# Strassen's seven products for the output product of eight token tiles in a fused attention and bilinear feed-forward kernel

## The chip, the cores and the metric

The kernel runs on one core of a Trainium2 chip. The metric is the device time of one execution in microseconds. A program on one core has single runs; a run counts as slow when it lies over 1.5% above the fastest run of the same kernel. A median quoted here is over all runs, as recorded; where one of them was slow, the median without it stands beside it. Ratios and verdicts (faster, same, slower at 2%, or unclear) come from the fast runs alone, of the same rounds on the same chip, with a 95% interval.

## The reference

```python
scores = scale * np.matmul(q, k.transpose(0, 1, 3, 2))     # q, k, v: 8 batches, 8 heads, 576 positions, 64
mask_local = (rel >= 0) & (rel < 32)                       # heads 0 to 3
mask_strided = (rel >= 0) & (pos[None, :] % 32 == pos[:, None] % 32)   # heads 4 to 7
... # masked softmax
x = attn_out.transpose(0, 2, 1, 3).reshape(4608, 512)
a = x @ w_a                                                # 512 -> 1536
b = x @ w_b
out = (a * b) @ w_out                                      # 1536 -> 512, float32
```

## The kernel before

The 4608 tokens are worked off in 9 tiles of 512. A tile has 16 slots: 12 for blocks of 128 hidden features (two products, then the multiply into `pf`), and 4 for 128 tokens each of the output product. The attention of the next batches is strewn into the slots as steps S (scores), V (values and normalising, which writes `xT`, the input of the products) and D (transposes of k and q on VectorE, then transfers on the sync engine's queue). The kernel fixes the order of each engine's instructions itself (`manual_schedule`); the order below is therefore part of the design. PSUM is the memory that matmuls write to; it is used here in banks of 512 float32 columns.

```python
def ffn_ab(t, f, mid, ab=None):
    ...                                     # 4 + 4 matmuls of 512 columns into two PSUM banks
    a_sb = fsb.tile([128, TTOK], F32, tag="a_sb", name="a_sb")
    nc.scalar.copy(a_sb, ab[0])
    nc.vector.tensor_mul(pf[:, f, :], a_sb, ab[1])

def ffn_y(t, j, mid):
    ...
        y = psum4["mm"].tile([128, n], F32, tag="mm", name="mm")
        for f in range(FD):                 # 12 matmuls of 512 columns
            nc.tensor.matmul(y, lhsT=pf[:, f, 128 * j:128 * (j + 1)], rhs=wo_sb[:, f, c0:c0 + n],
                             start=(f == 0), stop=(f == FD - 1))
        ...                                 # copy to SBUF, one store of 128 rows

# a V step from batch 2 on: ScalarE makes 1/sum, VectorE multiplies it into xT
nc.scalar.activation(r, sums, ACT.Ln)
nc.scalar.activation(r, r, ACT.Exp, scale=-1.0)
for j in range(2):
    ...
    nc.vector.tensor_mul(dst[:, W * half:W * (half + 1)], o[:64, j, :W], r[:, j])

# the slots of the attention steps from batch 3 on, and of the transposes from batch 4 on
LATER = {-2: "S0", -1: "S1", 0: "V0", 1: "S2", ... 10: "V5", 11: "S7", 12: "V6", 13.5: "V7"}
gs = ... (3, 5, 7, 9, 11, 12, 13, 14, 15, 17)
```

The softmax here doesn't subtract the row's maximum and nothing guards it: scores larger than these inputs give would overflow.

Of the kernel before, what the change touches and what calls it, by code (L numbers as in the profile page):

```python
# [7 lines left out]
F32 = mybir.dt.float32  # L8
BF16 = mybir.dt.bfloat16
I16 = mybir.dt.int16  # L10
ALU = mybir.AluOpType
# [12 lines left out]
PW = 344  # L24
VW = 128
WCH = (0, 2, 5, 8, 10, 12)


@with_exitstack
def kernel(  # L30
# [10 lines left out]
    nc = tc.nc  # L41
    B, H, S, D = q.shape
    assert (B, H, S, D) == (8, 8, 576, 64)
    scale = 1.0 / (D ** 0.5)
    d_model = H * D
    n_tok = B * S
    d_ff = moe_w_a.shape[1]
    KD = d_model // 128
    FD = d_ff // 128
    TTOK = 512  # L50
    NT = n_tok // TTOK
    HL = H // 2
    W = S // 2

    const = ctx.enter_context(tc.tile_pool(name="const", bufs=1))
    wp = ctx.enter_context(tc.tile_pool(name="weights", bufs=1))
    nat = ctx.enter_context(tc.tile_pool(name="nat", bufs=1))
    sb = ctx.enter_context(tc.tile_pool(name="sb", bufs=3))
    fsb = ctx.enter_context(tc.tile_pool(name="ffn", bufs=2))
# [3 lines left out]
    psum4 = {}  # L63
# [90 lines left out]
                             rhs=nc.const_aps.tensor(1.0, [128, 224], BF16), start=True, stop=True)  # L154

    cur = {}
    xT = const.tile([128, KD, n_tok], BF16)
    wa_sb = wp.tile([128, KD, d_ff], BF16)
    wb_sb = wp.tile([128, KD, d_ff], BF16)
    wo_sb = wp.tile([128, FD, d_model], BF16)  # L160

    tl = {}

# [2 lines left out]


    nats = {}

    def load_qk(b, strided, heads=range(HL), names="kq"):  # L170
        for nm in names:
            src = {"k": k, "q": q}[nm]
            if b < FIRST_D:
                n, R, h0 = (NP, RS, HL) if strided else (96, RL, 0)
                if (b, nm, strided) not in nats:
                    nats[b, nm, strided] = nat.tile([n, HL, R, D], BF16, tag=f"{nm}{R}", name=f"{nm}{R}", bufs=1)
                t = nats[b, nm, strided]
                hs = slice(heads[0], heads[-1] + 1)
                nc.gpsimd.dma_start(out=t[:, hs], in_=src[b, h0:h0 + HL].rearrange("h (p r) d -> p h r d", r=R)[:, hs])
            elif strided:  # L180

                t = nat_s[nm]
                n = 32 if b == FIRST_D else YS
                for h in heads:
                    nc.gpsimd.dma_start(  # L185
                        out=t[32 * h:32 * h + n],
                        in_=bass.AP(tensor=src.tensor, offset=(b * H + HL + h) * S * D,
                                    ap=[[RS * D, n], [YS * RS * D, 3], [1, RS * D]]))
            else:
                if 0 in heads:  # L190
                    nats[b, nm, strided] = nat.tile([128, NY, D], BF16, tag=f"{nm}l", name=f"{nm}l")
                t = nats[b, nm, strided]
                for h in heads:
                    nc.gpsimd.dma_start(out=t[32 * h:32 * h + 32],  # L194
                                        in_=src[b, h].rearrange("(i y) d -> y i d", y=32))
            nats[b, nm, strided] = t
# [127 lines left out]
    ps = {}  # L324
# [102 lines left out]
    def step_VT(b, u):  # L427

        c, half, M, n, G = unit(u)
        p = ps.pop((b, u))  # L430
        o = psum4["o"].tile([128, 2, 512], F32, tag="o", name="o")
        for i in range(G):
            for j in range(2):
                if c < 2:
                    vt = vl_buf[b % 2][:, (2 * c + j) * 6 + 3 * half + i]
                else:
                    vt = vs_buf[b % 2][:, 2 * (c - 2) + j, 4 * half + i]
                nc.tensor.matmul(o[:, j, i * n:(i + 1) * n], lhsT=vt, rhs=p[:M, j, i * n:(i + 1) * n], start=True, stop=True)  # L438

        r = sb.tile([128, RS * 4 * D], BF16, tag="xr", name="xr", bufs=2)[:64, :4 * W].bitcast(F32)  # L440
        r = r.rearrange("p (j w) -> p j w", j=2)
        if c < 2:
            sums = o[64:, :, :W]
        else:

            sums, r = (t.rearrange(e, p=NP) for t, e in ((o[64:, :, :W], "d j (g p) -> d j p g"), (r, "d j (p g) -> d j p g")))
        nc.scalar.activation(r, sums, ACT.Ln)  # L447
        nc.scalar.activation(r, r, ACT.Exp, scale=-1.0)  # L448
        for j in range(2):
            dst = xT[64 * j:64 * j + 64, c, S * b:S * (b + 1)]  # L450
            if c < 2:
                nc.vector.tensor_mul(dst[:, W * half:W * (half + 1)], o[:64, j, :W], r[:, j])  # L452
            else:
                nc.vector.tensor_mul(dst.rearrange("d (p r) -> d p r", r=RS)[:, :, G * half:G * (half + 1)],  # L454
                                     o[:64, j, :W].rearrange("d (g p) -> d p g", p=NP), r[:, j])
# [10 lines left out]
    def X_e(b, c):  # L466
        n = LW if c < 2 else NP
        tp = held.pop((b, "x", c))
        tv = tp.rearrange("d (g p) -> d g p", p=n)
        dst = xT[:, c, S * b:S * (b + 1)]  # L470
        if c >= 2:
            dst, tv = dst.rearrange("d (p r) -> d p r", r=RS), tv.rearrange("d g p -> d p g")
        else:
            tv = tp
        if (b, c) == (0, 3):
            nc.vector.tensor_copy(dst[:, :NP // 2], tv[:, :NP // 2])
            nc.scalar.copy(dst[:, NP // 2:], tv[:, NP // 2:])
        else:
            nc.scalar.copy(dst, tv)
# [30 lines left out]

    pfs = {}

    def ab_mm(t, f, ab, kks, mid=None, first=0, last=KD - 1):
        for w, ps_ in zip((wa_sb, wb_sb), ab):
            if mid and ps_ is ab[1]:
                mid()
            for kk in kks:
                nc.tensor.matmul(ps_, lhsT=w[:, kk, 128 * f:128 * (f + 1)], rhs=xT[:, kk, TTOK * t:TTOK * (t + 1)],  # L518
                                 start=(kk == first), stop=(kk == last))

    def ffn_ab(t, f, mid, ab=None):
        if f == 0:
            pfs[t] = fsb.tile([128, FD, TTOK], BF16, tag="pf", name="pf", bufs=1)
        pf = pfs[t]
        if ab is None:
            ab = [psum4["mm"].tile([128, TTOK], F32, tag="mm", name="mm") for _ in range(2)]
            if f == 0:

                late = 1 if t == 1 else 3
                ab_mm(t, f, ab, [kk for kk in range(KD) if kk != late], last=-1)  # L530
                ab_mm(t, f, ab, [late], first=-1, last=late)
            else:
                ab_mm(t, f, ab, range(KD), mid)
        a_sb = fsb.tile([128, TTOK], F32, tag="a_sb", name="a_sb")
        nc.scalar.copy(a_sb, ab[0])  # L535
        nc.vector.tensor_mul(pf[:, f, :], a_sb, ab[1])  # L536
        return pf[:1, f, :1]

    def ffn_y(t, j, mid):
        pf = pfs[t]  # L540

        c0 = 0
        for z, n in enumerate((256, 128, 128) if (t, j) == (NT - 1, 3) else (d_model,)):
            y = psum4["mm"].tile([128, n], F32, tag="mm", name="mm")
            for f in range(FD):
                nc.tensor.matmul(y, lhsT=pf[:, f, 128 * j:128 * (j + 1)], rhs=wo_sb[:, f, c0:c0 + n],  # L546
                                 start=(f == 0), stop=(f == FD - 1))
                if f == FD // 2 - 1:
                    mid()
            y_sb = fsb.tile([128, n], F32, tag="y_sb", name="y_sb", bufs=3)  # L550
            act = t < NT - 1 or (j + z) % 2 == 1
            (nc.scalar.copy if act else nc.vector.tensor_copy)(y_sb, y)  # L552
            r0 = TTOK * t + 128 * j
            (nc.scalar if z == 2 else nc.sync).dma_start(out=out[r0:r0 + 128, c0:c0 + n], in_=y_sb)
            c0 += n
        return y_sb[:1, :1]


    with tc.manual_schedule(engines={ENG.PE, ENG.SP, ENG.Pool, ENG.DVE, ENG.Activation}):
# [28 lines left out]
        first = {}  # L588
        for nm in ORDER:
# [27 lines left out]
            elif nm[0] == "F":  # L617
                f = int(nm[1])
# [10 lines left out]
        open_psum(ctx, mm=3, tp=1, o=1)  # L629
        slots = []  # L630
        for t in range(NT):
            slots += [(ffn_ab, t, f) for f in range(FD)] + [(ffn_y, t, j) for j in range(4)]
        steps = {}
        for b in range(1, B):
            for pos, names in (STEPS.get(b) or {16 * (b - 1) + x: n for x, n in LATER.items()}).items():
# [2 lines left out]
        def take(pos):  # L638
            for b, names in steps.get(pos, ()):
                run(b, names)  # L640
# [3 lines left out]
        def do(i, fn, *args):  # L644
            at.setdefault(i, []).append(lambda: fn(*args))
# [24 lines left out]
        do(17, rezero, 1)  # L670
        for i, t in ((0, vl_buf[0]), (0, vs_buf[0]), (18, vl_buf[1]), (19, vs_buf[1])):
            do(i, fill_v, t)
        for i, (fn, t, j) in enumerate(slots):
            mid = lambda: take(i - 0.5)
            done = fn(t, j, mid) if fn is ffn_y else fn(t, j, mid, first.get(j) if t == 0 else None)
            if i > 13 and i in at:

                nc.gpsimd.tensor_copy(pace, done)  # L678
            take(i)
            for f in at.get(i, ()):  # L680
                f()
# [28 lines left out]
```

## Time and profile before

| | before |
|---|---|
| median of the first 3 runs | 343.59 us (342.35 to 344.39) |
| span of the profiled run | 341.5 us |
| TensorE (PE) busy | 98% |
| VectorE (DVE), ScalarE (ACT) busy | 60%, 60% |
| GpSimd (POOL) busy | 41% |
| a tile with attention (tiles 3 to 5) | 35.45 us, of it the output product 11.40 |
| tile 7, without attention | 31.08 us, of it the output product 10.36 |

A busy TensorE is the bound here, because hardly any idle time stands before its matmuls.

### The profile page before, as it was taken

To read this page: it belongs to the slowest core of one execution; us is meant where nothing else is said; L and a number is where in the kernel's file an instruction comes from. 1 tells how busy PE (TensorE), PEld (TensorE's weight loads), DVE (VectorE), ACT (ScalarE), POOL (GpSimd) and SP (SyncE) were. 2 spreads that over 40 slices of the span, in tenths; PEclk is the share of its full clock that TensorE was granted. 3 is DMA by queue.
4 is the path that set the end of the run, shared out by engine and by line. 5 is a ranking of instruction groups with operands and counts; after the bars stand their busy time and mean duration, and the time that the engine had idled before them with its cause. 6 is when DMAs were issued, how large, how long until landed. Compare 5 with 4: busy or idle time off the path is not lost.

```text
span 341.5 us, 6887 instructions
## 1 busy us (share of the span) xinstructions
PE 333.1 (98%) x2520; PEld 173.7 (51%) x2520; DVE 205.1 (60%) x400; ACT 203.9 (60%) x331; POOL 140.4 (41%) x247
## 2 busy tenths in 40 slices
PE   8999999989989999999999999999999999999995
PEld 6754555445545555555555555555555444444444
DVE  6866657758759766876578846885666333303331
ACT  5754865368767765876587657775688533223311
POOL 8945539898537434653465346633000000000000
PEclk9999999999999999999999999999999999999999
DMA  9999999997999599969997989888220110021002
GB/s 160 154 203 197 202 176 172 179 154 89 129 200 101 90 99 185 99 110 91 165 104 133 77 168 96 132 80 145 76 59 2 61 63 0 0 92 34 0 31 94
DMA packets 102242, 37.56 MB, mean 110 GB/s; under 512 B 77632, under 2 KB 97728, under 8 KB 102208
## 3 DMA queue, kind: packets, MB, share of 16 engines
q0 software_dynamic: 87760, 19.58, 63.7%
q1 hardware_dynamic: 14304, 17.47, 16.2%
q8 instruction: 20, 0.33, 0.4%
q14 instruction: 14, 0.11, 0.1%
q10 hardware_dynamic: 144, 0.07, 0.1%
HBM read 39.71 MB, written 9.44 MB: 144 GB/s over the span
## 4 chain that ended last, share of the span: by engine, by line
PE 70%; DMA 17%; SPq 3%; DVE 3%; ACT 3%; POOL 2%; issue 2%; DVEq 0%; ACTq 0%
PE mm L518 41%; PE mm L546 20%; DMA vl<-in_v_dram 4%; PE o L438 3%; PE st L340 3%; DMA k<-in_k_dram 3%; DMA wa_sb<-in_moe_w_a_dram 3%; SPq L302 2%; DMA qz01l<-tq 2%; PE misc L153 2%; DMA out_dram<-y_sb 1%; DMA qz01s<-tq 1%; ACT xr L447 1%; DMA qz11s<-tq 1%; DVE tq L283 1%
## 5 line engine op out<-in xcount | busy, mean ns | idle before, releaser
L518 PE MATMUL mm<-xT,wb_sb 128*128 128x512 bf16 x424 | 110.1, 379 | 0.3
L518 PE MATMUL mm<-xT,wa_sb 128*128 128x512 bf16 x424 | 110.2, 379 | 0.1
L536 DVE TENSOR_TENSOR pf<-a_sb,mm 128x512 bf16<-128x512 f32 x106 | 71.9, 678 | 48.3 <-PE mm L518 25.5
L546 PE MATMUL mm<-wo_sb,pf 128*128 128x512 bf16 (+2 forms) x456 | 99.6, 368 | 0.1
L535 ACT COPY a_sb<-mm 128x512 f32<-128x512 f32 x106 | 62.1, 586 | 45.4 <-PE mm L518 43.0
L518 PEld LDWEIGHTS <-wb_sb 128*128 128x128 bf16 x432 | 41.7, 98 | 49.5 <-issue 1.3
L546 PEld LDWEIGHTS <-pf 128*128 128x128 bf16 x456 | 41.5, 98 | 42.3 <-issue 0.4
L518 PEld LDWEIGHTS <-wa_sb 128*128 128x128 bf16 x432 | 38.1, 98 | 34.2 <-issue 0.2
L552 ACT COPY y_sb<-mm 128x512 f32<-128x512 f32 (+2 forms) x35 | 20.0, 571 | 46.6 <-PE mm L546 38.6
L348 ACT ACTIVATE p<-st 128x576 bf16<-128x576 f32 (+1 forms) x64 | 41.7, 651 | 8.8 <-PE st L340 8.2
L447 ACT ACTIVATE xr<-o 64x576 f32<-64x576 f32 x48 | 31.1, 647 | 23.5 <-PE o L438 23.3
L454 DVE TENSOR_TENSOR xT<-o,xr 64x288 bf16<-64x288 f32 x48 | 21.6, 450 | 33.1 <-ACT xr L448 32.8
L448 ACT ACTIVATE xr<-xr 64x576 f32<-64x576 f32 x48 | 32.8, 682 | 1.5
L452 DVE TENSOR_TENSOR xT<-o,xr 64x288 bf16<-64x288 f32 x48 | 21.6, 450 | 16.9 <-ACT xr L448 16.4
L678 POOL CAST pace<-pf 1x1 f32<-1x1 bf16 x51 | 11.6, 227 | 41.5 <-DVE pf L536 41.3
L358 DVE TENSOR_TENSOR p<-p,mask_l 128x576 int16<-128x576 int16 x32 | 14.6, 455 | 17.1 <-ACT p L348 17.1
L218 POOL DMA_DIRECT2D vs<-in_v_dram x24 | 19.6, 817 | 9.9 <-issue 9.9
L194 POOL DMA_DIRECT2D kl<-in_k_dram x24 | 16.0, 666 | 6.7 <-issue 5.0
L194 POOL DMA_DIRECT2D ql<-in_q_dram x24 | 16.0, 666 | 6.6 <-DMA wo_sb<-in_moe_w_out_dram 3.8
L185 POOL DMA_DIRECT2D natk<-in_k_dram x24 | 14.6, 610 | 3.6 <-issue 3.0
L185 POOL DMA_DIRECT2D natq<-in_q_dram x24 | 14.6, 609 | 0.0
L678 POOL COPY pace<-y_sb 1x1 f32<-1x1 f32 x22 | 4.2, 189 | 24.2 <-ACT y_sb L552 24.2
(116 smaller groups left out, 316.2 us busy)
## 6 DMA issues: line engine op xcount, KB each, us to landing
out_dram<-y_sb SPq DMA_DIRECT2D x35, 256.0 KB, 2.4
vl<-in_v_dram POOLq DMA_DIRECT2D x7, 384.0 KB, 6.6
kl<-in_k_dram POOLq DMA_DIRECT2D x24, 72.0 KB, 2.8
ql<-in_q_dram POOLq DMA_DIRECT2D x24, 72.0 KB, 3.3
vs<-in_v_dram POOLq DMA_DIRECT2D x24, 72.0 KB, 3.6
wo_sb<-in_moe_w_out_dram POOLq DMA_DIRECT2D x4, 384.0 KB, 11.9
natk<-in_k_dram POOLq DMA_DIRECT2D x20, 72.0 KB, 3.3
natq<-in_q_dram POOLq DMA_DIRECT2D x20, 72.0 KB, 3.3
```

Source lines behind the costliest of these rows:

```text
L185: nc.gpsimd.dma_start(out=t[32 * h:32 * h + n], in_=bass.AP(tensor=src.tensor, offset=(b * H + HL + h) * S * D, ap=[[RS * D, n], [YS * RS ...
L194: nc.gpsimd.dma_start(out=t[32 * h:32 * h + 32], in_=src[b, h].rearrange("(i y) d -> y i d", y=32))
L348: nc.scalar.activation(p[:M, :, :W], st[:M, :, :W], ACT.Exp, scale=scale)
L447: nc.scalar.activation(r, sums, ACT.Ln)
L448: nc.scalar.activation(r, r, ACT.Exp, scale=-1.0)
L452: nc.vector.tensor_mul(dst[:, W * half:W * (half + 1)], o[:64, j, :W], r[:, j])
L454: nc.vector.tensor_mul(dst.rearrange("d (p r) -> d p r", r=RS)[:, :, G * half:G * (half + 1)], o[:64, j, :W].rearrange("d (g p) -> d p g", ...
L518: nc.tensor.matmul(ps_, lhsT=w[:, kk, 128 * f:128 * (f + 1)], rhs=xT[:, kk, TTOK * t:TTOK * (t + 1)], start=(kk == first), stop=(kk == last))
L535: nc.scalar.copy(a_sb, ab[0])
L536: nc.vector.tensor_mul(pf[:, f, :], a_sb, ab[1])
L546: nc.tensor.matmul(y, lhsT=pf[:, f, 128 * j:128 * (j + 1)], rhs=wo_sb[:, f, c0:c0 + n], start=(f == 0), stop=(f == FD - 1))
L552: (nc.scalar.copy if act else nc.vector.tensor_copy)(y_sb, y)
```

## The change

Its intent is to save an eighth of the output product. Each tile's 512 tokens are halved (runs of 16 tokens go alternately to one half and the other), as are the 1536 hidden features and the 512 outputs. Strassen's scheme then needs seven products of half size instead of eight, and pays with sums of the inputs, of the weights and of the results. Sums of `pf` go to VectorE. With A for the four quarters of `pf` (tokens by hidden features) and B for those of `wo_sb`, the products are M1 = (A11 + A22)(B11 + B22), M2 = (A21 + A22)B11, M3 = A11(B12 - B22), M4 = A22(B21 - B11), M5 = (A11 + A12)B22, M6 = (A21 - A11)(B11 + B12) and M7 = (A22 - A12)(B21 + B22), which is subtracted. They run in the order M3, M4, M1, M2, M5, M6, M7 and share four PSUM banks: M2 is added onto M4, M5 onto M3 and M6 onto M1. To make room in SBUF, `xT` becomes a ring of four batches and the sums share a buffer with the first batches' loads. All products from tile 1 on, the plain ones too, now go round four banks instead of three.

```diff
+FAST_Y = (1, 2, 3, 4, 5, 6, 7, 8)
-    xT = const.tile([128, KD, n_tok], BF16)
+    xT = const.tile([128, KD, XR * S], BF16)          # XR = 4
+    wf = wp.tile([128, 5, FG, HN], BF16, name="wf")   # five sums of weights, ten VectorE instructions
 ...
+    def mm_bank(shape):                               # every fourth bank is the one of pool "tp"
 ...
+        if t in FAST_Y:                               # pf is written with the two halves apart
+            nc.vector.tensor_mul(pf[:, f, :].rearrange("p (i a s) -> p a i s", i=2, s=16), halves(a_sb), halves(ab[1]))
+    def fast_s(t, n, gs):                             # n = 0, 1, 2: sums for M1; for M5 and M2; for M6 and M7
+        ...
+            nc.vector.tensor_tensor(s[:, :, 0:HT], x[:, :, 0, 0], x[:, :, 1, 1], op=ALU.add)
 ...
+    def y_plan(t):
+        def post(k):                                  # after the last matmul of product k
+            if k == "3":   nc.scalar.copy(v["a"], bank["a"])
+            elif k == "4": nc.vector.tensor_tensor(v["w"], bank["b"], v["a"], op=ALU.add)
+            elif k == "1": nc.vector.tensor_tensor(v["e"], bank["c"], v["w"], op=ALU.add)
+            elif k == "2": nc.scalar.copy(v["y21"], bank["b"]); store(v["y21"], 1, 0)
+                           nc.gpsimd.tensor_tensor(v["h"], v["w"], v["y21"], op=ALU.subtract)
+            elif k == "5": nc.scalar.copy(v["y12"], bank["a"]); store(v["y12"], 0, 1)
+                           nc.gpsimd.tensor_tensor(v["g"], v["e"], v["y12"], op=ALU.subtract)
+            elif k == "6": nc.vector.tensor_tensor(v["y22"], bank["c"], v["h"], op=ALU.add); store(v["y22"], 1, 1)
+            else:          ...                        # y11 = g - bank["d"]
+        for k, b, lhs, rhs in (("3", "a", ...), ("4", "b", ...), ("1", "c", ...),
+                               ("2", "b", ...), ("5", "a", ...), ("6", "c", ...), ("7", "d", ...)):
+            ...                                       # 2 x 6 matmuls of 256 columns each
 ...
+        for t in FAST_Y:
+            for n, at_ in ((0, (3, 7, 11)), (1, (4, 8, 11)), (2, (5, 9, 11))):
+                for z in range(3):
+                    do(16 * t + at_[z], fast_s, t, n, slice(2 * z, 2 * z + 2))
```

## The prediction

> **What bounds the kernel now.** I read the head of the page first, to see which engine has no idle time left.
>
> ```profile
> span 341.5 us, 6887 instructions
> PE 333.1 (98%) x2520; PEld 173.7 (51%) x2520; DVE 205.1 (60%) x400; ACT 203.9 (60%) x331; POOL 140.4 (41%) x247
> ```
>
> TensorE (PE) is busy for 98% of the span at a granted clock of 0.998, and every other engine for 60% or less. Since a busy PE need not be at its peak, I next read the groups of the three large products and took the distance from one matmul's start to the next from the single records of the trace.
>
> ```profile
> L518 PE MATMUL mm<-xT,wb_sb 128*128 128x512 bf16 x424 | 110.1, 379 | 0.3
> L518 PE MATMUL mm<-xT,wa_sb 128*128 128x512 bf16 x424 | 110.2, 379 | 0.1
> L536 DVE TENSOR_TENSOR pf<-a_sb,mm 128x512 bf16<-128x512 f32 x106 | 71.9, 678 | 48.3 <-PE mm L518 25.5
> L546 PE MATMUL mm<-wo_sb,pf 128*128 128x512 bf16 (+2 forms) x456 | 99.6, 368 | 0.1
> ```
>
> Matmuls overlap, so 379 ns is a latency. The start to start distance is 216 ns for 512 columns, 109 ns for 256 and 56 ns for 128 (the narrow ones are the last block of the output product). The idle time before these groups is 0.5 us in all: the sequence of matmuls is the kernel's length, and weight loads hide behind matmuls even at 56 ns. A saving in matmul columns is thus a saving in time, as long as nothing makes PE wait. So the third view is the table by stretches: tile 3's two hidden products (134.61 to 158.67), its output product (to 170.07), then the same two stages of tile 7, which has no attention beside it.
>
> ```profile
> 134.61:158.67 24.06, 23.98 (x185) 12.54 (x183) 18.22 (x34) 19.10 (x31) 12.91 (x26) 1.00 0.96 106
> 158.67:170.07 11.40, 11.40 (x83) 5.74 (x80) 6.57 (x13) 5.82 (x11) 5.02 (x10) 1.00 0.82 146
> 275.67:296.39 20.72, 20.72 (x97) 9.37 (x96) 7.56 (x11) 7.62 (x13) 0.00 (x0) 1.00 0.04 13
> 296.39:306.75 10.36, 10.36 (x49) 4.70 (x48) 0.69 (x1) 1.76 (x3) 0.00 (x0) 1.00 0.20 76
> ```
>
> After the length, the columns are PE, weight loads, DVE (VectorE), ACT (ScalarE) and POOL (GpSimd). The 60% of the page is an average over two regimes: with attention, VectorE is busy for 18.22 + 6.57 = 24.8 of 35.5 us; in tiles 7 and 8 for 8.3 of 31.1. Last, the timeline of VectorE where an output product starts (158.67):
>
> ```profile
> 156.91 0.64 DVE L536 TENSOR_TENSOR pf<-a_sb,mm 128x512 bf16<-128x512 f32 x1
> 158.28 0.91 DVE L454 TENSOR_TENSOR xT<-o,xr 64x288 bf16<-64x288 f32 x2 [0.72 <-ACT xr L448]
> 159.22 0.69 DVE L536 TENSOR_TENSOR pf<-a_sb,mm 128x512 bf16<-128x512 f32 x1
> 159.83 0.45 DVE L358 TENSOR_TENSOR p<-p,mask_s 72x576 int16<-72x576 int16 x1
> 160.20 0.70 DVE L288 STREAM_TRANSPOSE tk<-natk 128x512 bf16<-128x512 bf16 x1
> 163.51 0.91 DVE L454 TENSOR_TENSOR xT<-o,xr 64x288 bf16<-64x288 f32 x2 [2.61 <-ACT xr L448]
> 164.45 1.46 DVE L288 STREAM_TRANSPOSE tk<-natk 128x512 bf16<-128x512 bf16 x2
> ```
>
> VectorE works in program order, and the normalising multiplies into xT wait for ScalarE. The holes (0.72 us every 4 us in the first stage, 2.61 us here) are all there is for new work.
>
> **What the Trainium skill says.** "TensorE: Matmul & The Clock Gate", section "Wait — 56ns, not 53.3ns?": a warm matmul starts every N ÷ 2.4 GHz plus about 2.5 ns. That is 215.8, 109.2 and 55.8 ns, and the trace agrees (216, 109, 56), so halving the width costs next to nothing. "VectorE: DVE Perf Modes", section "The perf-mode tier table (the rule you actually need)": a two-input elementwise operation runs at double rate on bf16 in SBUF, and at single rate with a PSUM operand. The trace agrees: 455 ns for the 16-bit mask with 576 elements, 678 ns for 512 with PSUM. "GPSIMD Engine Reference", section 3.1: about 2.6 cycles per element for such an operation; with the 1.2 GHz of its specifications I estimate 1.1 us for 512 float32 elements. No row of the trace shows one.
>
> **The change part by part.**
>
> *Output product.* A tile's 48 matmuls of 512 columns (48 x 216 ns = 10.37 us) become 7 products x 2 row blocks x 6 = 84 of 256 columns (84 x 109 ns = 9.16 us): 1.21 us less per tile, 9.7 us for eight tiles. Tile 4 now straddles the end of the ring in xT, so its 96 matmuls of 512 become 192 of 256: 96 x 2 ns = +0.2 us.
>
> *VectorE.* From the fit of the mask row (576 elements, half as many cycles, 455 ns) a sum of 512 bf16 elements is about 0.42 us and one of 1024 about 0.69 us. Nine sums a tile: 3 x 0.42 + 6 x 0.69 = 5.4 us. Four combinations from PSUM at 0.69 us: 2.8 us. So 8.2 us a tile, 65 us in eight, plus ten weight sums of 768 elements (0.55 us each, 5.5 us) in tile 1. In a tile with attention 24.8 + 8.2 = 33.0 us must fit into 35.5 - 1.2 = 34.3 us. Where an instruction follows another without a wait, the next starts some 80 ns before the last one's end (mask, then transpose above: 159.83 and 160.20), so it is not quite 96%; but the holes for ScalarE don't all close.
>
> *Others.* ScalarE does 3 copies instead of 4, GpSimd gets two subtractions of an estimated 1.1 us per tile, each store becomes two. All lie beside other work, except at the end.
>
> *What lands on the path.* In the first stage of a steady tile the sums take 2 x (0.42 + 0.69 + 0.69) = 3.6 us, less about 0.5 us of overlap, and the holes in those slots give about the same. Going through the changed order by hand with the durations above, each multiply into pf ends by at most 0.6 us before its PSUM bank is needed (there are four banks now, two pairs), and VectorE enters the output stage about 0.7 us late. So PE is not held there. The output stage is different. The seven products share four banks: product M2 is added into the bank of M4, so it waits until VectorE has read M4. With zero at the start of that stage, PE does M3, M4, 8 attention matmuls (0.27 us) and M1, and wants M2 at about 4.2 to 4.4 us. VectorE, in its order: xT pair, last pf multiply (ends 2.0), mask (2.3), transpose (3.0), three sums of the last third (3.3, 3.9, 4.5), the next xT pair (5.5, its ScalarE input being ready at about 4.3), a transpose (6.2), and only then M4's read (6.8). PE stands still for about 2.5 us, plus 0.2 us where M4 needs the last pf. So the stage takes 11.4 - 1.2 + 2.7 = 12.9 us: a steady tile gets 1.5 us longer.
>
> *Sum over tiles.* Tiles 2 to 5: 4 x 1.5 = +6.0. Tile 6 has no transposes left, M4's read ends at about 5.7 us, a wait of 1.5 us: +0.3. Tile 7: after the last pf (ends 0.75) and three sums (2.4) the read follows M4's end at once: -1.2. Tile 8: -1.2, but the tail gets longer, since M6's and M7's results leave in five stores on one queue rather than one last small store on another: about +0.6, so -0.6. Tile 1: the weight sums come on top. In its slots with sums, VectorE needs some 18.7 us where PE needs 13.9; the two-pair slack takes about 2, leaving +2.7; its output stage gains 1.2, loses about 3.6, and gets back the 1.4 us that PE now waits there for a DMA (93.5 us in the trace): +1.0; together +3.7. Ring cut +0.2; the shared load buffer, which makes the second batch's loads wait for all the first's transposes, +0.2. Sum: 6.0 + 0.3 - 1.2 - 0.6 + 3.7 + 0.2 + 0.2 = +8.6 us. I take a little off, because I was pessimistic for tile 1: 343.6 + 7.7 = 351.3 us.
>
> **The rivals.**
>
> *The matmul saving comes through.* If M4's read slipped in early enough, 343.6 - 9.7 + 0.8 = about 335 us. For it speaks that PE is the bound and that tiles 7 and 8 must show the gain; against it the fixed order, in which two multiplies that wait for ScalarE and a transpose stand ahead of that read.
>
> *VectorE becomes the bound of the whole middle.* If the sums missed the double rate, a sum of 1024 would take about 1.2 us instead of 0.69: some 4 us more per tile, in five tiles without room: about 370 us. Against it speaks that the mask with two free dimensions has the rate.
>
> *GpSimd comes late.* M6's read waits for a subtraction on GpSimd, which stands behind transfers it issues (0.6 to 1.5 us each). I see about 2 us of slack; without it, another 1 us per tile, about 356 us.
>
> **Range and chances.** My main term is five or six waits of 2 to 3 us; half a microsecond of error in each is 3 us, tile 1 is worth another 2 and the tail 1. Hence 344.5 to 358. The limit of slower by 2% is 350.5 us, just under my value: slower 0.55, within 2% 0.40, faster (under 336.7 us) 0.05.
>
> **What would show it.** Right: matmuls of 256 columns 109 ns apart; sums near 0.42 and 0.69 us; VectorE above 80% of the span; in each tile with attention a gap of 2 to 3 us in PE before M2, ended by VectorE's read of M4, and none in tiles 7 and 8, whose output stage is 9.2 us. Wrong: no such gap, or one before another product; matmuls of the hidden products waiting for pf in tiles 2 to 5; sums at 1.2 us; a wait for GpSimd ahead of M6.

## The result, and the profile after

| | before | after |
|---|---|---|
| median of 4 runs | 343.74 us | 356.01 us (355.24 to 357.19) |
| ratio of the fast runs | | 1.0354 (1.032 to 1.0388), slower |
| span of the profiled run | 341.5 us | 353.0 us |

A ratio is the mean time of one kernel's fast runs over that of the other's of the same rounds, so it is not quite the ratio of the medians quoted here. The time lies within the predicted range, 4.7 us above the predicted value.

The head of the page of the changed kernel:

```profile
span 353.0 us, 7811 instructions
PE 327.3 (93%) x2855; PEld 211.0 (60%) x2886; DVE 265.2 (75%) x513; ACT 200.8 (57%) x324; POOL 174.8 (50%) x290
```

TensorE has less to do (327.3 instead of 333.1 us of modelled busy time) and now stands idle for 7% of a longer span. The table by stretches of the changed kernel says where: tile 3's hidden products and output stage, then the same for tile 7 (columns: length, PE, weight loads, DVE, ACT, POOL, granted clock, transfers).

```profile
139.97:164.08 24.11, 23.75 (x176) 12.36 (x179) 22.03 (x42) 18.59 (x30) 13.77 (x27) 1.00 1.03 124
164.08:176.53 12.45, 10.37 (x119) 9.25 (x115) 9.62 (x19) 5.80 (x10) 7.10 (x12) 1.00 0.66 95
287.17:307.89 20.72, 20.61 (x96) 9.37 (x96) 11.51 (x18) 7.02 (x12) 2.89 (x7) 1.00 0.13 39
307.89:317.06 9.17, 9.17 (x85) 8.22 (x84) 4.39 (x7) 1.76 (x3) 2.90 (x3) 1.00 0.10 30
```

In tile 7 the output stage takes 9.17 us, 1.19 less than before: the products themselves give all they should. In tile 3 the first stage is as long as before (24.11 against 24.06), although VectorE is busy for 22.03 us of it, and the output stage is 1.05 us longer with 2.08 us of idle PE. The timeline of the changed kernel in tile 3's output stage (start, length, instruction) shows the wait:

```profile
165.03 0.69 DVE L565 TENSOR_TENSOR pf<-a_sb,mm 128x512 bf16<-128x512 f32 x1
...
166.63 0.38 DVE L578 TENSOR_TENSOR ps<-pf 128x512 bf16<-128x512 bf16 x1
...
166.93 0.68 DVE L580 TENSOR_TENSOR ps<-pf 128x1024 bf16<-128x1024 bf16 x1
...
167.53 0.68 DVE L582 TENSOR_TENSOR ps<-pf 128x1024 bf16<-128x1024 bf16 x1
...
168.23 0.91 DVE L470 TENSOR_TENSOR xT<-o,xr 64x288 bf16<-64x288 f32 x2
...
169.18 0.71 DVE L304 STREAM_TRANSPOSE tk<-natk 128x512 bf16<-128x512 bf16 x1
...
169.81 0.65 DVE L611 TENSOR_TENSOR ya<-mm,ya 128x512 f32<-128x512 f32 x1
...
170.52 2.02 PE L650 MATMUL mm<-wo_sb,ps 128*128 128x256 bf16 x17 [2.08 <-DVE ya L611]
```

L611 is VectorE's read of M4, and the matmul at 170.52 is the first of M2. From the last matmul of M1 to it there are 2.24 us too many, start to start; the excess is 2.24 us in each of tiles 2 to 5, and 1.65 us in tile 6. ("Excess" means this below: the time from one matmul's start to the next, less what it is when nothing waits.) No other wait of more than 0.6 us stands in tiles 2 to 5.

Tile by tile, from one tile's first hidden product to the next:

| tile | 0 | 1 | 2 | 3 | 4 | 5 | 6 | 7 | 8 to end |
|---|---|---|---|---|---|---|---|---|---|
| before | 40.85 | 39.33 | 35.92 | 35.46 | 35.45 | 35.45 | 34.70 | 31.08 | 34.78 |
| after | 41.69 | 42.34 | 37.18 | 36.56 | 38.81 | 36.89 | 34.94 | 29.89 | 35.97 |
| difference | +0.8 | +3.0 | +1.3 | +1.1 | +3.4 | +1.4 | +0.2 | -1.2 | +1.2 |

With +0.3 us before tile 0 this is the whole 11.5 us between the spans. Tile 4 is worse than its neighbours for another reason, which its output stage shows in the same view (the clock is the last column but two):

```profile
201.02:215.34 14.32, 12.19 (x118) 10.24 (x116) 9.78 (x19) 5.79 (x11) 7.28 (x12) 0.88 0.60 88
```

For 3.4 us of it, right after the wait before M2, the granted clock was half. Matmuls of 256 columns then start 213 ns apart. The same happened in tile 1. Added up over the matmuls, each of the two stretches cost about 1.6 us. The changed kernel's runs differ in this: the one with a mean clock of 0.998 took 355.24 us, the three with 0.987 to 0.988 took 356.4 us on average; their spans differ less, 353.3 against 354.0 us, and one run is too few to tell. The kernel before is not free of it: of its 8 runs beside the first experiments, two had a mean clock of 0.985 and 0.990 and took 347.8 and 347.3 us, the others 343.1 to 345.2 us.

### The profile page after: what moved, and what is told of

Its sections match the earlier page's. It is cut to its first block, busy times and chain, and to the rows that moved or that the text cites. A ratio compares the mean times of both kernels' runs of the same rounds, so it can differ in the third digit from the quotient of the medians.

```text
span 353.0 us, 7811 instructions
## 1 busy us (share of the span) xinstructions
PE 327.3 (93%) x2855; PEld 211.0 (60%) x2886; DVE 265.2 (75%) x513; ACT 200.8 (57%) x324; POOL 174.8 (50%) x290
## 4 chain that ended last, share of the span: by engine, by line
PE 56%; DMA 17%; DVE 14%; issue 4%; POOL 3%; ACT 2%; SPq 2%; POOLq 0%; DVEq 0%
PE mm L545 33%; PE mm L650 15%; DMA vl<-in_v_dram 4%; DMA shared<-in_k_dram 3%; PE st L356 3%; DMA wa_sb<-in_moe_w_a_dram 3%; PE o L454 3%; DVE xT L470 2%; DVE pf L565 2%; DMA qz11s<-tq 2%; DMA qz01l<-tq 2%; PE misc L154 2%; SPq L318 2%; DVE tk L304 2%; DMA natk<-in_k_dram 1%
## 5 line engine op out<-in xcount | busy, mean ns | idle before, releaser
L545 PE MATMUL mm<-xT,wb_sb 128*128 128x512 bf16 (+1 forms) x465 | 108.9, 357 | 0.3
L545 PE MATMUL mm<-xT,wa_sb 128*128 128x512 bf16 (+1 forms) x451 | 107.6, 356 | 1.3 <-DVE xT L470 0.3
L565 DVE TENSOR_TENSOR pf<-a_sb,mm 128x512 bf16<-128x512 f32 x96 | 65.1, 679 | 20.9 <-PE mm L545 15.5
L822 POOL CAST pace<-pf 1x1 f32<-1x1 bf16 x78 | 23.9, 306 | 93.6 <-DVE pf L565 92.8
L650 PEld LDWEIGHTS <-ps 128*128 128x128 bf16 x486 | 47.6, 101 | 19.1 <-issue 12.9
L364 ACT ACTIVATE p<-st 128x576 bf16<-128x576 f32 (+1 forms) x64 | 41.6, 650 | 15.3 <-PE st L356 14.7
L650 PE MATMUL mm<-wf,ps 128*128 128x256 bf16 (+1 forms) x294 | 35.5, 270 | 0.9 <-DVE y_sb L637 0.9
L650 PE MATMUL mm<-wo_sb,ps 128*128 128x256 bf16 x192 | 26.2, 293 | 10.6 <-DVE ya L611 10.6
L650 PE MATMUL mm<-wf,pf 128*128 128x256 bf16 x192 | 23.8, 273 | 1.5 <-DVE pf L565 1.5
L650 PEld LDWEIGHTS <-pf 128*128 128x128 bf16 x192 | 17.8, 98 | 4.6 <-DVE pf L565 2.1
L617 ACT COPY y_sb<-mm 128x512 f32<-128x512 f32 x8 | 4.7, 585 | 26.8 <-PE mm L650 26.8
## 6 DMA issues: line engine op xcount, KB each, us to landing
wo_sb<-in_moe_w_out_dram POOLq DMA_DIRECT2D x4, 384.0 KB, 11.9
```

What stands on the lines that cost most here:

```text
L364: nc.scalar.activation(p[:M, :, :W], st[:M, :, :W], ACT.Exp, scale=scale)
L545: nc.tensor.matmul(ps_[:, c0:c0 + n], lhsT=w[:, kk, 128 * f:128 * (f + 1)], rhs=xT[:, kk, x0:x0 + n], start=(kk == first and c0 == 0), sto ...
L565: nc.vector.tensor_mul(pf[:, f, :].rearrange("p (i a s) -> p a i s", i=2, s=16), halves(a_sb), halves(ab[1]))
L650: nc.tensor.matmul(bank[b][:, q, n], lhsT=lhs(g, q), rhs=rhs(g)[:, n], start=new and q == 0 and g == 0, stop=g == FG - 1, skip_group_check ...
L822: nc.gpsimd.tensor_copy(pace, done)
```

## The experiments

Theory A is the prediction's: M2 waits because VectorE's read of M4 stands too far back in its queue. Rival B is that VectorE is simply full in the tiles with attention, so that any order gives the same. All experiments start from the changed kernel unless said otherwise, and all gave correct results.

**1. V6 half a slot later.**

```diff
-LATER = {... 12: "V6", 13.5: "V7"}
+LATER = {... 12.5: "V6", 13.5: "V7"}
```

> One attention step of tiles 2 to 6 (V6, whose result VectorE multiplies into xT) is issued half a slot later, after VectorE's read of M4 instead of ahead of it. Nothing else changes, VectorE has the same instructions. Theory A (the order of VectorE's queue in the output stage holds product M2): of the 2.24 us that PE waits before M2 in tiles 2 to 5, the pair of xT multiplies (0.9 us) goes, the sums and one transpose stay ahead of the read, so the wait falls to about 1.3 us; in tile 6 from 1.65 to about 0.6 us. Sum about -4.7 us: near 351.3 us. Rival B (VectorE is simply full, whatever its order): no change, 356 us, the wait turns up somewhere else.

Measured: 351.79 us median (351.46 without a slow run of 357.05), ratio to before 1.0192 (1.0118 to 1.0266), which leaves "slower by 2%" unclear. The same VectorE instructions in another order take 4.2 to 4.6 us less than in the changed kernel. The excess before M2 fell to 1.12 to 1.25 us in tiles 2 to 5, and to below 0.3 us in tile 6, so the output stages became 11.6, 11.6, 11.6 and 12.2 us. But some of the gain went at another place. The timeline of this kernel in tile 3's first stage:

```profile
149.74 0.51 SPq L318 DMA_DIRECT2D qz01s<-tq  x1
...
150.59 0.19 PE L356 MATMUL st<-qz00s,kT0s 128*128 128x72 bf16 x1 [2.06 <-DMA qz01s<-tq]
```

A score step waits for the last of ten transfers that bring the transposed q into place. They go out one after the other on one queue, some 0.6 us apart, from the moment VectorE has done its last transpose. Before the change PE reached this step at about the time the transfers landed (excesses of 0.2 us in tiles 3 to 5); M2's wait hid them in the changed kernel. In tile 3, 4 and 5 the first stage grew by 1.6 to 2.7 us over before.

**2. The whole order of the output stage.** As 1, and:

```diff
-gs = (3, 5, 7, 9, 11, 12, 13, 14, 15, 17)
+gs = (3, 5, 7, 9, 13, 13, 14, 15, 15, 17)
-... (2, (5, 9, 11)))        # slots of the sums for M6 and M7
+... (2, (5, 9, 13)))
```

> As e1, and the transposes of slots 11 and 12 go to 13, and the third sum of the last third (needed only by M6) goes behind the reads of M4 and M1. VectorE does the same instructions in another order. Theory A: M4's read ends about 3.7 us after the start of the stage, before M2 is due (4.2), so the wait before M2 in tiles 2 to 6 is gone (below 0.2 us): 4 x 2.24 + 1.65 = -10.6 us, and a little more where the clock throttle had set in after the waits: near 345 us, level with the kernel before. Rival B (VectorE is full): the time stays above 352 us, with new waits of PE for pf or for M6's and M7's reads.

Measured: 361.65 us, ratio 1.0483 (1.0401 to 1.0564), 10 us slower than experiment 1 and against both theories' wording: the wait before M2 did fall to 0.5 to 0.6 us, and a new one of 3.2 to 3.4 us stood before M6. The timeline of this kernel in tile 2's output stage:

```profile
133.84 3.30 DVE L582 TENSOR_TENSOR ps<-pf 128x1024 bf16<-128x1024 bf16 x1
...
134.09 1.28 POOL L620 TENSOR_TENSOR ya<-ya,y_sb 128x512 f32<-128x512 f32 x1
...
135.31 1.27 POOL L626 TENSOR_TENSOR ye<-ye,y_sb 128x512 f32<-128x512 f32 x1
...
137.20 0.50 PE L650 MATMUL mm<-wf,ps 128*128 128x256 bf16 x3 [3.08 <-DVE ps L582]
```

The moved sum took 3.30 us instead of 0.68, in each of the four tiles. This is not the whole loss: in this profile the clock also fell to half for 3.4 us after the wait before M6 in tiles 2 and 5, and the four runs had a mean clock of 0.969 to 0.985. The 2.62 us more are the length of GpSimd's two subtractions, 2.55 us. The Trainium skill, "SBUF — State Buffer", section "Who interferes with whom", says that a VectorE instruction with two SBUF inputs contends with a GpSimd instruction that reads SBUF, as its second input comes through an interface that the two engines share. So theory A got a second half, A': GpSimd's subtractions hold up the sum that I had moved beside them. Experiments 5 and 6 test it.

**3. Strassen only in tiles 7 and 8.**

```diff
-FAST_Y = (1, 2, 3, 4, 5, 6, 7, 8)
+FAST_Y = (7, 8)
```

> Strassen only in tiles 7 and 8, which have no attention beside them; the weight sums, the ring in xT and the shared load buffer stay. Theory A: tile 7 -1.2 us, tile 8 +1.2 us (its tail as in the changed kernel), tile 0 +0.8, start +0.3, ring +0.2, weight sums in tile 1 up to +1: 344.5 to 346 us, so 10 us of the loss lie in tiles 1 to 6 and come back. Rival C (the loss is mostly in the overheads that all tiles share: loads, ring, tail): stays above 350 us.

Measured: 344.72 us, ratio 0.9998 (0.9934 to 1.0062), as theory A has it. The loss sits in tiles 1 to 6. The weight sums still run in tile 1 here; that tile took 39.5 us against 39.3 before, so they cost little by themselves.

**4. A PSUM bank for each of the last pieces of M7.**

```diff
+                    if tail and q == 1:
+                        bank[b], new = mm_bank([128, 2, HN]), True
```

> The changed kernel, but in the last tile the three last pieces of M7 have a PSUM bank each instead of one for all. Theory A: PE no longer waits for VectorE's reads of the same bank (0.57 and 0.38 us in the trace), the stage after 337.8 us gets about 0.9 us shorter: 355.1 us. Rival: the end is set by the queue of stores, which leave one after the other, then less than 0.3 us comes of it.

Measured: 355.79 us, ratio 1.0327 (1.0254 to 1.0399), no gain that these runs can tell. The two waits are gone from the trace, and VectorE's last combination ends 9.7 us after the start of the last output stage instead of 10.9. The end does not come earlier: the stage takes 16.0 us instead of 15.3. In the changed kernel, this is the last tile's end:

```profile
344.48 5.50 SPq L603 DMA_DIRECT2D out_dram<-y_sb  x8
...
347.03 0.49 PE L650 MATMUL mm<-wf,ps 128*128 128x128 bf16 x6 [0.57 <-DVE y_sb L637]
...
347.90 0.49 PE L650 MATMUL mm<-wf,ps 128*128 128x128 bf16 x6 [0.38 <-DVE y_sb L637]
```

The queue of stores is busy until 12.2 us after the start of the stage here, and until 12.6 us in experiment 4. So the gain is what the rival expects, and the waits for the bank set nothing; whether it is the queue that does is taken up in experiment 7. The lists of the stores of the kernel before and of the changed one (shortest, median and longest issue in ns) show that each issue takes longer now:

```profile
L554 SPq DMA_DIRECT2D out_dram<-y_sb x37: 332/338/527, 48.8 to 337.8; - x37
```

```profile
L603 SPq DMA_DIRECT2D out_dram<-y_sb x65: 603/604/755, 97.7 to 349.4; - x65
```

A store of the changed kernel writes 8 runs of 16 rows that lie apart, 1 KB of each row; before, it wrote 128 whole rows. There are nine of them at the end, and the last is issued at 349.4 us.

**5. The moved sum back ahead of M4's read.** As 2, without its last edit, so the sum runs before GpSimd has anything to subtract.

> As e2_order (which took 361.65 us, against what was expected), but the third sum of the last third is again ahead of M4's read, so it runs before GpSimd's two subtractions start. Theory A': e2 lost because that sum, with two SBUF inputs, stood still for 2.6 us while GpSimd's subtractions ran (3.30 us instead of 0.68, 4 times), and PE waited for it before M6. Then that wait of 3.3 us is gone in all four tiles, the wait before M2 stays at 0.5 us or less (it ended with GpSimd's read of M3's copy), the output stages of tiles 2 to 5 take 10.7 to 11.3 us, and the time is about 349 us, of which some 3 to 4 us are waits for the transfers of the transposed q that had been hidden behind M2's wait. Rival B (VectorE is full): no less than e1's 351.8 us, a new wait in the output stage.

Measured: 349.99 us, ratio 1.0148 (1.0066 to 1.0231), unclear at 2%, close to what A' expects. The wait before M6 is gone. The wait before M2 was 1.04 to 1.25 us, more than I had expected, and the output stages took 11.5 to 11.9 us instead of 10.7 to 11.3. That rest is not VectorE's own work, as the timeline of this kernel in tile 3's output stage shows:

```profile
166.33 1.80 POOL L822 CAST pace<-pf 1x1 f32<-1x1 bf16 x1
...
168.08 0.82 POOL L234 DMA_DIRECT2D vs<-in_v_dram  x1
...
169.10 0.69 DVE L611 TENSOR_TENSOR ya<-mm,ya 128x512 f32<-128x512 f32 x1 [1.01 <-POOL pace L822]
```

M4's read overwrites the copy of M3, so it must wait until GpSimd has read that copy to pace its loads. GpSimd is late: its reading of a single element of `pf` took 1.80 us while VectorE ran its three sums (0.17 us at 164.77), and it then issued a load first. Experiment 10 takes GpSimd's reading of M3's copy away (and the two subtractions too, so it does not test the reading alone).

**6. Experiment 2 with the two subtractions on VectorE.**

```diff
-                nc.gpsimd.tensor_tensor(v["h"], v["w"], v["y21"], op=ALU.subtract)
+                nc.vector.tensor_tensor(v["h"], v["w"], v["y21"], op=ALU.subtract)
-                nc.gpsimd.tensor_tensor(v["g"], v["e"], v["y12"], op=ALU.subtract)
+                nc.vector.tensor_tensor(v["g"], v["e"], v["y12"], op=ALU.subtract)
```

> e2_order with the two subtractions moved from GpSimd to VectorE, nothing else. VectorE gets 1.4 us more per tile to do. Theory A' (GpSimd's subtractions hold the late sum up): the late sum takes 0.68 us again and PE's wait before M6 falls from 3.3 to below 1 us; some of that is given back by the longer queue: 351 to 356 us, faster than e2 although VectorE does more. Rival B (VectorE is full): slower than e2's 361.65 us, as VectorE has 8 x 1.4 us more.

Measured: 348.12 us (346.93 without one slow run), ratio 1.0082 (1.0001 to 1.0163). VectorE has 1.4 us more to do in each of eight tiles, and the kernel is 13.5 us faster than experiment 2. In the timeline of this kernel the sum is back at its length, and PE's wait is short:

```profile
134.83 0.65 DVE L582 TENSOR_TENSOR ps<-pf 128x1024 bf16<-128x1024 bf16 x1
...
135.40 0.68 DVE L620 TENSOR_TENSOR ya<-ya,y_sb 128x512 f32<-128x512 f32 x1
...
135.54 1.70 PE L650 MATMUL mm<-wf,ps 128*128 128x256 bf16 x14 [0.39 <-DVE ps L582]
```

This shows A' and speaks against rival B. It went further than my 351 to 356 us: four times 2.6 us of the held sum are 10.5 us, and the fast runs here had a mean clock of 0.996 to 0.998, against 0.969 to 0.985 in experiment 2.

**7. The last tile's stores on two queues.** As 4, with every second store of the last tile issued by ScalarE.

```diff
-                nc.sync.dma_start(out=rows[:, :, i, z, n], in_=y[:, z, n])
+                v["s"] = v.get("s", 0) + 1
+                (nc.scalar if t == NT - 1 and v["s"] % 2 == 0 else nc.sync).dma_start(...)
```

> e4_tail_bank with every second store of the last tile issued by ScalarE's queue. Theory: the end was set by the stores, nine of them in 6.6 us on one queue; with two queues the last store leaves soon after VectorE's last combination (346.8 us in e4), and the end comes 2 to 3 us earlier: 353 us against 355.8. Rival (the transfers themselves are slow, not their issue): less than 0.5 us.

Measured: 356.94 us (355.45 without one slow run), ratio 1.0348 (1.0239 to 1.0458). A miss for the theory. ScalarE's first store took 1.45 us to issue and stood ahead of its copy of M5's result, which came 0.9 us later in the stage than in experiment 4; so the last combinations came later too. The last store was issued 10.9 us after the start of the stage instead of 12.0, but the wait for the landings ended at 15.3 us (15.1 in experiment 4). The traces keep the transfers themselves, and they speak for the rival: the table by stretches from the last store's issue to the end of its transfers, for the changed kernel and for this one, ends in the rate in GB/s.

```profile
349.98:351.80 1.82, 0.00 (x0) 0.00 (x0) 0.00 (x0) 0.00 (x0) 0.00 (x0) 0.80 0.47 151
```

```profile
349.28:352.48 3.20, 0.00 (x0) 0.00 (x0) 0.00 (x0) 0.00 (x0) 0.00 (x0) 0.70 0.50 154
```

With every store issued, data still move for 1.8 and for 3.2 us, at much the same rate. Here is that rate in 40 slices over the last stores, for the kernel before (330.9 to 340.0 us) and for the changed one (343.8 to 352.0 us):

```profile
GB/s 0 0 0 9 342 405 351 45 0 0 0 0 0 72 54 306 369 324 27 9 9 18 27 9 0 0 72 405 351 324 0 270 293 16 236 50 0 99 189 0
```

```profile
GB/s 0 0 0 0 0 0 75 65 100 200 190 170 175 195 145 155 155 180 155 140 155 150 170 150 160 170 160 170 175 180 190 185 185 180 180 162 167 100 30 0
```

Some 1.05 MB move in both. The stores of whole rows do it in bursts of up to 405 GB/s with pauses between them, those of the new form at no more than 200 GB/s without a pause. So a second queue for the issues gained nothing. What in the new form lowers the rate (rows of 1 KB instead of 2, or the order of the rows) was not separated by a run.

**8. Tiles 6, 7 and 8, with the edits of 1, 4 and 7.**

> Strassen in tiles 6, 7 and 8 only, with the later V6 of e1 and the tail of e7. Theory A: -1.1, -1.2 and -1.2 us for the tiles, nothing lost in the tail, +0.5 us for the ring, the shared load buffer and the weight sums: near 341 us (340 to 342.5), about 1% faster than before. Later V6 might cost or gain a little in tiles 2 to 5. Rival: the gain is eaten by the weight sums in tile 1 and the loads: 343.5 us or more.

Measured: 344.41 us, ratio 1.0008 (0.9935 to 1.008). Tiles 6 and 7 gave 0.9 and 1.2 us as expected (33.79 and 29.89 us), but the last tile's output stage took 16.5 us, against 14.1 before, and tile 1 with the weight sums 39.9 us, 0.5 more than before. Theory A missed those two; the time is the rival's.

**9. Tiles 6 and 7, plain last tile, weight sums in tiles 4 to 6.**

```diff
-FAST_Y = (1, 2, 3, 4, 5, 6, 7, 8)
+FAST_Y = (6, 7)
-                do(17 + 2 * n + z, fast_w, n, slice(3 * z, 3 * z + 3))
+                do((66, 69, 72, 75, 82, 85, 88, 91, 97, 98)[2 * n + z], fast_w, n, slice(3 * z, 3 * z + 3))
```

with the later V6 of experiment 1.

> Strassen in tiles 6 and 7 alone, with the later V6, the weight sums spread over tiles 4 to 6 instead of tile 1, and the last tile with the plain product and its old stores. Theory: tile 6 -0.9 to -1.1 us (33.6 to 33.8 against 34.7), tile 7 -1.2, last tile's output stage back at 14.1 us, tile 1 within 0.3 us of before, start and tile 0 up to +0.6 us: 341.5 to 342.5 us, about 0.5% faster than before. Rival (the ring and shared buffer cost as much as two tiles give): 343.5 us or more.

Measured in 5 rounds: 342.35 us against 344.34 us for the kernel before in the same rounds, ratio 0.9948 (0.9909 to 0.9987): faster by half a per cent. Tile 1 took 39.2 us, and the last tile's output stage 13.9 us. Not all of the gain is Strassen's. In the profiled run (340.50 us, the fastest of the six) tiles 6 and 7 gave 2.1 us and the start took 1.1 us more, but tiles 2 to 5, which have the plain product here, also took 1.0 us less than before, in sum. In experiments 3 and 8 they took 0.8 and 0.9 us less. The fourth PSUM bank may be the reason; no run separates it.

**10. Tiles 2 to 7 with everything learned.** The order of 5, the subtractions of 6 on VectorE, tile 1 and the last tile plain, and GpSimd's pacing read moved from M3's copy to `pf`:

```diff
-FAST_Y = (1, 2, 3, 4, 5, 6, 7, 8)
+FAST_Y = (2, 3, 4, 5, 6, 7)
-        return v[("a", "e", "y12", "y11")[j]][:1, 0, :1]
+        return pfs[t][:1, FD - 1, :1] if j == 0 else v[("a", "e", "y12", "y11")[j]][:1, 0, :1]
```

> Strassen in tiles 2 to 7, with what the runs have taught: later V6, transposes after M4's read, the sums before it, the two subtractions on VectorE so that GpSimd holds up no sum, and GpSimd's pacing read no longer on M3's copy, so that M4's read doesn't wait for GpSimd. Tile 1 and the last tile are plain. Theory A: the output stages of tiles 2 to 5 take 10.3 to 10.7 us (11.4 before), PE waits less than 0.4 us before M2, and 0.5 to 1 us per tile is lost to the transfers of transposed q; tiles 6 and 7 -1.1 and -1.2: 340.5 to 342 us. Rival B (VectorE is full): the waits for pf and for q in the first stages grow by more than 1 us per tile, and the time is 343.5 us or more.

Measured in 5 rounds: 342.53 us (342.37 without one slow run), ratio 0.9947 (0.9916 to 0.9978), just above what theory A expects and below rival B's range. The stretches of this kernel's tile 3:

```profile
134.93:159.91 24.98, 23.79 (x177) 12.37 (x180) 23.08 (x44) 18.59 (x30) 12.44 (x26) 1.00 1.03 128
159.91:170.40 10.49, 10.38 (x119) 9.16 (x116) 9.11 (x19) 5.80 (x10) 6.75 (x11) 1.00 0.72 97
```

In tile 3 PE is busy for 10.38 of the 10.49 us of the output stage: no wait before M2 is left, with more work on VectorE than the changed kernel had. The output stages of tiles 2 to 5 took 10.5 to 10.7 us, as theory A has it. The first stage lost 0.9 us to the transfers of transposed q. Compared with experiment 9, where tiles 2 to 5 have the plain product, the four output stages gained 3.0 us in sum and the four first stages lost 3.8; PE's waits before the scores that need transposed q add up to 4.5 us there. So experiments 9 and 10 beat the kernel before by half a per cent and the changed kernel by 4%, and Strassen in the four steady tiles with attention brought nothing in these profiles, even in the mended order.

What could not be tried: giving the sums a buffer of their own, to see what the shared load buffer costs. It did not fit; the last pool asked for 28 KB per partition, and some 15 KB were left.

## Why the prediction was right, and where it was off

*The products themselves.* Right. 256 columns take 109 ns, the stage of tile 7 takes 9.17 us (9.16 worked out), and tile 7 got 1.19 us shorter (1.21).

*The sums.* Right: 0.38 us and 0.68 us in the median (0.42 and 0.69), the weight sums 0.53 us (0.55). The rival with sums at single rate fell with that.

*The first stages of steady tiles.* Right: PE waited for no `pf` in tiles 2 to 5, and these stages took 24.1 to 24.5 us, as before.

*The wait before M2.* The mechanism was right, and experiments 1, 2 and 10 show it: when the pair of 0.91 us ahead of M4's read left, the wait shrank by 1.0 to 1.1 us; when the transposes and a sum left too, it was 0.5 to 0.6 us; with GpSimd out of the way it was gone. The size was a little off, 2.24 us instead of 2.7 with the wait for the last `pf`, because VectorE entered the stage 0.4 us earlier than I had worked out: the last `pf` ended 1.64 us after the start of the stage (2.0 predicted), the sums at 4.13 (4.5), M4's read at 6.38 (6.8). Tiles 2, 3 and 5 got 1.1 to 1.4 us longer (1.5).

*Tile 6 and tile 1.* Tile 6: +0.2 us (+0.3). Tile 1: +3.0 us (+3.7, from which I had then taken a little off for pessimism). That these two are near each other is luck, for the pieces are not those predicted. The first stage, where the weight sums run, was to lose 2.7 us; it took 25.06 us against 25.29 before, 0.2 less, with one wait of 1.1 us. The output stage was to lose 1.0 us and lost 3.2 (17.29 against 14.04): PE waited there for late `pf` (0.6 and 1.2 us), for VectorE's multiply into `xT` (1.1 us) and before M2 (1.0 us), 3.9 us in sum where 3.6 were predicted, and about 1.6 us was the half clock, which no step had. The earlier wait for a transfer at the end is absorbed, as described.

*The tail.* This step failed: "it gets longer ... about +0.6, so -0.6". The last tile's output stage took 15.25 us against 14.06 before, so with 1.2 us saved the tail costs 2.4 us instead of 0.6. I had counted the stores and their queue, but with the old issue time of 332 ns and the old rate; a store of the new form takes 603 ns to issue, and its data move at no more than 200 GB/s instead of up to 405. The last store's issue ends 12.2 us after the start of the stage, and its data move until 14.0 us (12.3 in the kernel before). Experiment 7 speaks for the transfers as the limit, and not the issue. Besides, two pieces of M7 in one bank made PE wait, which I had not seen, though experiment 4 shows that this alone sets nothing.

*What no step had.* The clock fell to half for 3.4 us in two of the output stages with waits. In the profiled run tile 4's output stage is 1.9 us longer than tile 3's with it; what it costs over the runs is not known well (0.7 to 1.2 us, see above). And in the profiled run the start and tile 0 cost 1.1 us instead of 0.2: the first output product waits for the last weights 0.9 us longer (1.13 against 0.25 us of excess at 47 us), in a stretch where the transfers are busy throughout. The shared buffer, which reorders the early loads, is a likely cause, but it was only argued. Over the eleven profiles of kernels with that buffer, tile 0 ended 0.7 us later on average than in the one profile of the kernel before, in the single ones between 0.05 us earlier and 1.45 us later.

*A sign that was wrong.* VectorE was to be busy for over 80% of the span; it was 75%. The prediction's own sum (205.1 + 65 + 5.5 us in 351 us) gives 78%, so the sign did not follow from it.

*The rivals.* Rival 1 (the saving comes through) holds where there is no attention. In experiment 10, where the order was mended, it holds in the output stages, but the first stages lose it again. Rival 3, GpSimd late ahead of M6's read, did not come about. But GpSimd mattered in a way that I had not thought of: its subtractions held up VectorE's instructions with two SBUF inputs. In the changed kernel they already did so, harmlessly, with a mask of 0.45 us:

```profile
174.95 1.27 POOL L626 TENSOR_TENSOR ye<-ye,y_sb 128x512 f32<-128x512 f32 x1 [0.86 <-ACT y_sb L623]
...
175.39 1.14 DVE L374 TENSOR_TENSOR p<-p,mask_l 128x576 int16<-128x576 int16 x1 [0.25 <-ACT p L364]
```

The value was thus 4.7 us too low. In the profiled run the loss was 11.5 us, 2.9 more than the sum of 8.6: 1.8 in the tail, 0.9 in the start with tile 0, 1.0 in tiles 2 to 5 (where the half clock outweighs the shorter waits), and 0.7 less in tile 1. To this come the 0.9 us that I had taken off, and 0.9 us between the spans of the two profiled runs and the medians.

## What to carry to other kernels

A product that accumulates onto another's PSUM bank turns the reader of that bank into a link of the chain on the bound engine; look at what stands ahead of that reader in its queue, and which of those wait for yet another engine, before counting the engine's spare time. When one such wait goes, look at once at what it had been hiding; here it was a queue of transfers that had landed just in time, and it took back all that the better order gained in the tiles with attention. Moving work beside another engine's is only free if the two do not share a port: the same instruction took 0.68 us at one place of the program and 3.30 at another.

## What the Trainium skill lacked or had wrong

- "SBUF — State Buffer", section "Who interferes with whom": that a VectorE instruction with two SBUF inputs contends with a GpSimd one agrees with experiment 2. Of VectorE's two-port modes the section says that whoever issues first gets the shared pair, and in general that the order of issue decides who blocks. Here the sum's record begins at 133.84 us and the first subtraction's at 134.09, yet the sum was held, and held again by the second subtraction at 135.31, until it ended at 137.14. Records on GpSimd are rough, so this is an observation and not a rule.
- "TensorE: Matmul & The Clock Gate", section "HAM oscillation — how this bites in real kernels", gives idle gaps of more than about 3.4 us as the danger, and the section after it, "A second HAM failure mode: psum-queue depth-cycling", frequent short idles, without a figure. In the profiled run the half clock came in two output stages, whose waits before M2 were 1.0 us (tile 1, with three more waits of 0.6 to 1.2 us in the 10 us before) and 2.24 us (tile 4), and it did not come in tiles 2, 3 and 5 after the same 2.24 us. Its length, 3.4 us, agrees with the window that the page's section "What's actually happening" gives (3413 ns).
- "GPSIMD Engine Reference", section 3.1, "Elementwise — side-by-side cycle accounting": the estimate from its 2.6 cycles per element was 1.1 us for 512 float32 elements; the trace has 1.27 us (1.26 to 1.29).
- On no page did I find what a store's form does to the time of its issue: 603 ns for 8 runs of 16 rows of 1 KB, 332 ns for 128 whole rows.
